# A gated-linear-attention, expert and GLU kernel on one core: attention products in float32 with turned outputs, other loads and another hand-over

## The chip, the core and the metric

The kernel runs on one core of a Trainium2 chip. The core has five engines with queues of their own, each of which runs its instructions in the order of the program: PE (TensorE: matrix products, whose weight loads are shown apart as PEld), DVE (VectorE), ACT (ScalarE), POOL (GpSimd) and SP (SyncE, which here only issues DMAs). The metric is the device time of one execution in microseconds (us), taken as the median of the runs.

## The reference, cut to what matters

```python
# gated linear attention: B=4, 8 heads, 768 steps, head size 48
f = 1.0 / (1.0 + np.exp(-f_logit))
for t in range(S):
    state = f[:, :, t, :, None] * state + np.einsum('bhd,bhe->bhde', k[:, :, t], v[:, :, t])
    y[:, :, t] = np.einsum('bhd,bhde->bhe', q[:, :, t], state)
x = y as 3072 tokens of 384
# one expert of 8 per token
e_idx = np.argmax(x @ w_gate, axis=1)
h = np.maximum(x[mask] @ w1[e], 0.0)          # 384 -> 1024
out[mask] = gate_w * eom * (h @ w2[e])        # 1024 -> 384
# a gated linear unit over all tokens
gate = 1.0 / (1.0 + np.exp(-(x @ w_gate)))    # 384 -> 1536
out = (gate * (x @ w_val)) @ w_out            # 1536 -> 384
```

## The kernel before

**Attention.** The tokens are cut into 24 units of 128 steps (`NU`, six to a batch). Queries, keys and decays arrive turned, with two heads down the partitions: rows 0 to 47 and 64 to 111 of a tile of 112 rows (`PD`), and four such pairs (`HP`) side by side. Per unit: `s_log` makes logarithms of the decays (ACT), `s_sum` their running sums (DVE, one scan per pair), `s_decay` the exponentials (ACT) and the products with keys and queries (`kT`, `qT`, on POOL). `s_part` and `s_part2` then cut keys and queries into a high and a low part of the type float32r, the queries of each head among zeros for the other head (`qbh`, `qbl`), so that `s_score` can make the scores of two heads at a time from three float32r products of 256 columns (units 0 to 2 take whole float32 tiles, `qw`, instead). `am` is the score under the causal mask. `s_turn` turns the keys (`pk`), `s_state` makes the chunk's addition to the state (`pM`, then `sn`), and `s_y` the output `pY` with tokens down the partitions: per head `am` by 48 columns of values, per pair `qT` by 96 columns of the state. `s_xt` turns the finished rows again (`px`) and `s_logit` makes the two sets of eight router logits (`plg`) from them. A float32 product stands in the trace as two weight loads and two MATMULs, a transposition as one.

**Routing.** After every group of tiles (`groups`) `route` finds each token's expert and its rank there with some twenty small DVE instructions, and `put_rows` writes the rows with indirect DMAs (POOL) to the experts' slots in DRAM (`xs_all`).

**Experts.** Nine passes: the early slots of expert 0 (`W0`), its other ones, then the seven other experts in the order of their loads, each with up to 512 tokens. A pass has eight units `f` of 128 hidden columns, each with nine products for `ph` and, two units later (`LAG`), nine for `po`, all in three float32r parts (`mm3`). SP loads the weights (`st`, three buffers), ACT and DVE split them (`w_hi`, `w_lo`) into a ring of slots that the expert before gives back. Beside this the weights of the last stage, which are doubles, are loaded (`stg`, by SP), rounded (`single`, on ACT, POOL and DVE) and split. At unit 1 of a pass `store_pass` copies the last pass's outputs (`yt`) and stores them; at unit 4 `put_ids` writes the token numbers (one element of 4 bytes per row) and `gather_rows` fetches rows for the pass after the next one.

**GLU.** Six groups of 512 tokens by twelve units; a unit has 18 products of 512 columns and 12 of 384. The outputs are scattered by indirect DMA.

The order on each engine is the order of the code (`manual_schedule`); the loop over `i` interleaves stages of several units, and the tile library sets the waits. The lines that the change touches are printed below.

Of the kernel before, what the change touches and what calls it, by code (L numbers as in the profile page):

```python
# [28 lines left out]
def kernel(  # L29
# [36 lines left out]
    EARLY = 18  # L66
    #: The first tile of the last group.
    LATE = 21
    #: The slots of expert 0 that the first EARLY tiles fill.
    W0 = 208  # L70
    #: The rows of a pair of heads: the second's start at half the partitions.
    PD = P // 2 + D
    NRING = 34
    NWARM = 16
    #: The units whose products take the keys and queries whole.
    WHOLE = 3
    #: The units from which the vector engine takes the keys' low parts.
    LOW = 21
    WARM = (2, 2)
    FILL = {-2: 2, -1: 4, 0: 4, 1: 2}  # L80
# [10 lines left out]
    id_all = drp.tile([NT + SLOT, 1], I32, name="id_all")  # L91
# [7 lines left out]
    wg16 = const.tile([P, KD, 2 * NE], F32, name="wg16")  # L99
    carry = const.tile([P, 1, NE], BF16, name="carry")  # L100
    #: Of each token: its number and its factor.
# [7 lines left out]
    flag = const.tile([1, 1], I32, name="flag")  # L109
    gc_all = const.tile([PD, NU, HP], F32, name="gc_all")  # L110
    bm = const.tile([PD, 2], F32, name="bm")
    zero = const.tile([P, 1], F32, name="zero")

    def constants():
# [4 lines left out]
        )  # L119
        nc.vector.tensor_tensor(out=tris, in0=tri, in1=ident, op=ALU.subtract)  # L120
        nc.vector.tensor_reduce(
            out=bm, in_=ident[0:PD, :].rearrange("p (j d) -> p j d", j=2), axis=AX.X, op=ALU.add
        )
        nc.vector.memset(onec, 1.0)
        nc.gpsimd.iota(e8[:, 0, :], pattern=[[-1, NE]], base=NE, channel_multiplier=0, allow_small_or_imprecise_dtypes=True)
        nc.vector.memset(carry, 0.0)
        # NT less a token's number: an empty slot's zeros stand for none.
        nc.gpsimd.iota(meta[:, :, 0].bitcast(I32), pattern=[[-P, NU]], base=NT, channel_multiplier=-1)
# [3 lines left out]
    def load_router():  # L132
        nc.sync.dma_start(wg16[:, :, 0:NE], moe_w_gate.rearrange("(k p) e -> p k e", p=P))
        nc.sync.dma_start(wg16[:, :, NE : 2 * NE], moe_w_output_gate.rearrange("(k p) e -> p k e", p=P))
# [4 lines left out]
    def choose(pool, lg, u0, n):  # L139
        """The expert of each token of n tiles (its one-hot row) and the token's factor."""  # L140
# [7 lines left out]
        nc.vector.tensor_reduce(out=m, in_=l, axis=AX.X, op=ALU.max)  # L148
        nc.vector.tensor_tensor(out=t, in0=l, in1=bc(m, NE), op=ALU.subtract)
        nc.scalar.activation(out=ex, in_=t, func=AF.Exp)  # L150
        nc.vector.tensor_tensor(out=sc, in0=l, in1=bc(m, NE), op=ALU.is_equal)
        nc.vector.tensor_tensor(out=sc, in0=sc, in1=e8b, op=ALU.mult)
        nc.vector.tensor_reduce(out=ms, in_=sc, axis=AX.X, op=ALU.max)
        nc.vector.tensor_tensor(out=oh, in0=sc, in1=bc(ms, NE), op=ALU.is_equal)

        factor = [
            lambda: nc.vector.tensor_tensor(out=ohf, in0=oh, in1=g, op=ALU.mult),
            lambda: nc.vector.tensor_reduce(out=sel, in_=ohf, axis=AX.X, op=ALU.add),
            lambda: nc.scalar.activation(out=eg, in_=sel, func=AF.Exp, scale=-1.0),
# [1163 lines left out]
```

## Time and profile before

| | us |
|---|---|
| median of 3 runs (1016.81 to 1018.68) | 1017.18 |
| span of the profiled execution | 1017.1 |
| PE busy in it | 976.9 (96%) |
| PE weight loads | 890.3 (88%) |
| DVE busy | 527.7 (52%) |
| ACT busy | 380.1 (37%) |
| POOL busy | 253.1 (25%) |

The profiled execution and the median agree to 0.1 us. Busy shares are means over stages of unlike kinds, and a busy PE may run at half its clock, so the stages have to be read one by one; PE's granted clock stands beside its busy time in the view of stretches.

### The profile page before, as it was taken

The page shows a single profiled execution, that of the slowest core. Times are in us where ns is not written, and L with a number is a line of the kernel's source. Part 1 is how long each engine was busy: PE and PEld are TensorE (multiplying, and loading weights), DVE is VectorE, ACT ScalarE, POOL GpSimd, SP SyncE. Part 2 cuts the span into 40 slices and gives each one's busy share as a digit, 9 for nine tenths or more (in the row PEclk, how much of TensorE's full clock was granted, in tenths as well). Part 3 has the DMA queues.
Part 4 walks back from the last instruction along what each step waited for, and adds up shares of the span by engine and source line. Part 5 has one row for each costly group of instructions (what it writes and reads, how often), then busy time and mean ns, then how long its engine had stood idle before and what let it go on. Part 6 is the DMA issues. An engine that isn't in the chain of part 4 may idle for free.

```text
span 1017.1 us, 13322 instructions
## 1 busy us (share of the span) xinstructions
PE 976.9 (96%) x4891; PEld 890.3 (88%) x4891; DVE 527.7 (52%) x1011; ACT 380.1 (37%) x729; POOL 253.1 (25%) x220
## 2 busy tenths in 40 slices
PE   8999999999998998989979999999999999999996
PEld 5899999999997787988978888888888888888886
DVE  8978867866344875777769723222223222222222
ACT  5655455443124554455535522222222122122211
POOL 6544354545110432434345200100100100100001
PEclk8755555555599899999999999999999999999999
DMA  8576454331167586576653200100100100000000
GB/s 196 173 242 197 125 154 133 93 107 55 45 137 162 163 223 162 132 245 205 209 118 111 92 1 1 63 1 1 63 1 1 63 1 1 32 1 5 27 1 34
DMA packets 57532, 96.00 MB, mean 94 GB/s; under 512 B 13258, under 2 KB 35186, under 8 KB 57458
## 3 DMA queue, kind: packets, MB, share of 16 engines
q1 hardware_dynamic: 54386, 85.60, 30.9%
q0 software_dynamic: 3072, 9.46, 2.4%
q8 instruction: 40, 0.66, 0.3%
q14 instruction: 34, 0.28, 0.1%
HBM read 68.35 MB, written 26.69 MB: 93 GB/s over the span
## 4 chain that ended last, share of the span: by engine, by line
issue 43%; PE 36%; DVE 7%; DMA 7%; ACT 3%; POOL 2%; SPq 0%; POOLq 0%; DVEq 0%; ACTq 0%
PE pY L586 6%; DMA st<-in_moe_w_dram 6%; PE pS L542 5%; PE pY L583 3%; PE plg L398 2%; PE ph L762 2%; PE pM L563 2%; PE ph L763 2%; PE ph L764 2%; PE po L762 2%; PE po L763 2%; PE po L764 2%; DVE w_lo L225 2%; POOL out_dram L964 2%; PE px L386 1%
## 5 line engine op out<-in xcount | busy, mean ns | idle before, releaser
L1082 DVE TENSOR_TENSOR hf<-pv,sg 128x512 f32<-128x512 f32 x72 | 49.8, 691 | 267.6 <-PE pv L764 266.5
L964 POOL DMA_INDIRECT out_dram<-ob,ids x24 | 23.6, 982 | 410.7 <-DVE ob L963 405.2
L1078 ACT ACTIVATE sg<-pg 128x512 f32<-128x512 f32 x72 | 43.0, 598 | 174.1 <-PE pg L764 174.1
L1085 ACT CAST hh<-hf 128x512 fp32r<-128x512 f32 x72 | 44.7, 621 | 160.3 <-DVE hf L1082 160.3
L225 DVE TENSOR_TENSOR w_lo<-st,w_hi 128x384 fp32r<-128x384 f32 (+1 forms) x112 | 78.2, 723 | 51.0 <-ACT w_hi L224 50.0
L763 PE MATMUL po<-w_lo,hh 128*128 128x384 f32 x288 | 97.1, 337 | 0.0
L762 PE MATMUL po<-w_hi,hh 128*128 128x384 f32 x288 | 97.0, 337 | 0.0
L764 PE MATMUL po<-w_hi,hl 128*128 128x384 f32 x288 | 96.8, 336 | 0.0
L762 PE MATMUL po<-hh,w_hi 128*128 128x208 f32 (+8 forms) x216 | 76.2, 353 | 19.4 <-ACT yt L935 16.4
L586 PE MATMUL pY<-v,am 128*128 128x48 f32 x384 | 89.2, 384 | 0.0
L586 PEld LDWEIGHTS pY<-v,am 128*128 128x128 f32 x384 | 88.6, 320 | 0.2
L763 PE MATMUL pg<-xt_lo,w_hi 128*128 128x512 f32 x216 | 85.3, 395 | 0.0
L762 PE MATMUL pg<-xt_hi,w_hi 128*128 128x512 f32 x216 | 85.0, 394 | 0.0
L764 PE MATMUL pg<-xt_hi,w_lo 128*128 128x512 f32 x216 | 85.0, 394 | 0.0
L763 PE MATMUL pv<-xt_lo,w_hi 128*128 128x512 f32 x216 | 85.0, 394 | 0.0
L762 PE MATMUL pv<-xt_hi,w_hi 128*128 128x512 f32 x216 | 84.9, 393 | 0.0
L764 PE MATMUL pv<-xt_hi,w_lo 128*128 128x512 f32 x216 | 84.8, 393 | 0.0
L224 ACT CAST w_hi<-st 128x384 fp32r<-128x384 f32 (+1 forms) x112 | 59.6, 560 | 66.9 <-DMA st<-in_moe_w_dram 52.5
L174 POOL TENSOR_SCALAR cva<-cva 128x512 f32<-128x512 f32 (+1 forms) x30 | 58.8, 1960 | 94.6 <-ACT cva L173 94.5
L762 PE MATMUL ph<-xt_hi,w_hi 128*128 128x208 f32 (+8 forms) x216 | 78.1, 362 | 2.9 <-DVE hl L1015 1.5
L763 PE MATMUL ph<-xt_lo,w_hi 128*128 128x208 f32 (+8 forms) x216 | 76.6, 355 | 0.0
L763 PE MATMUL po<-hl,w_hi 128*128 128x208 f32 (+8 forms) x216 | 74.8, 346 | 1.7 <-DVE hl L1015 1.7
(182 smaller groups left out, 2197.3 us busy)
## 6 DMA issues: line engine op xcount, KB each, us to landing
st<-in_moe_w_dram SPq DMA_DIRECT2D x48, 256.0 KB, 5.0
st<-in_moe_w_dram SPq DMA_DIRECT2D x32, 384.0 KB, 5.3
qk<-in_qkt_dram SPq DMA_DIRECT2D x48, 192.0 KB, 4.2
xs_all<-zrow SPq DMA_DIRECT2D x8, 772.0 KB, 4.9
yT_all<-zrow SPq DMA_DIRECT2D x21, 256.0 KB, 3.1
ft<-in_ft_dram SPq DMA_DIRECT2D x48, 96.0 KB, 4.6
v<-in_v_dram SPq DMA_DIRECT2D x24, 192.0 KB, 2.6
stg<-in_moe_w_gate_dram SPq DMA_DIRECT2D x9, 512.0 KB, 6.2
```

The costliest lines, as they stand in the source:

```text
L174: nc.gpsimd.tensor_scalar(out=af, in0=af, scalar1=HW_LEAST, scalar2=HW_MOST, op0=ALU.max, op1=ALU.min)
L224: nc.scalar.copy(hi, src)
L225: nc.vector.tensor_tensor(out=lo, in0=src, in1=hi.bitcast(F32), op=ALU.subtract)
L542: nc.tensor.matmul(pS[:, 2 * i : 2 * i + 2, :], lhsT=a, rhs=b, start=(n == 0), stop=(n == len(terms) - 1))
L586: nc.tensor.matmul(pY[:, h, :], lhsT=d["am"][:, h, :], rhs=vt[:, h, :], start=(c == 0), stop=True, skip_group_check=True,)
L762: nc.tensor.matmul(ps, lhsT=ah, rhs=bh, start=first, stop=False)
L763: nc.tensor.matmul(ps, lhsT=ah, rhs=bl, start=False, stop=False)
L764: nc.tensor.matmul(ps, lhsT=al, rhs=bh, start=False, stop=last)
L964: put = nc.gpsimd.indirect_dma_start(out=out[:, :], out_offset=bass.IndirectOffsetOnAxis(ap=idx[g][:, i : i + 1], axis=0), in_=ob, in_offs ...
L1078: nc.scalar.activation(out=sg, in_=pg, func=AF.Sigmoid)
L1082: nc.vector.tensor_tensor(out=hf, in0=pv, in1=sg, op=ALU.mult)
L1085: nc.scalar.copy(hh, hf)
```

## The change

The scores, the outputs and the state's part of them are now float32 products of one head each. `s_score` gives head `j` of a pair the rows 0 to 47 or 64 to 111 and a bank of its own; `s_y` makes the output turned (`pY[at, hp, :]`: 48 or 64 columns of weights from the values, 128 moving columns from `am`), so that its copy `xT` feeds the logits directly and `s_rows` turns it back for the rows. `s_part`, `s_part2` and their tiles go; `kT` moves from POOL to DVE; the scan is one instruction for all four pairs; the state is 48 columns per pair instead of 96. The start is written out, with units 0 and 1 ahead of the loop. `route` is cut into more steps, the groups are (6, 6, 5, 5, 2) tiles, and the rows for pass 0 are fetched, scaled and turned inside the attention loop. In the expert stage the staged loads go from three buffers to five (`NST`), the doubles are fetched from POOL's queue, the last addition of `single` goes from POOL to DVE, the stores of `yt` and of the token numbers come later and in pieces, and a token number is written with its row's last 16 words. The zero fills of `yT_all` and `id_all` and half of that of `xs_all` go.

```diff
     def route(u0, n):
...
+        some(first)
         yield
+        some(factor, 3)
+        yield
...
+    def s_rows(u):
+
+        px = bank_mm([P, HP, 2, P // 2], "px")
+        for hp in range(HP):
+            nc.tensor.transpose(
+                px[:, hp].rearrange("p j d -> p (j d)")[:, 0:PD], st[u]["xT"][:, hp, :], ident[0:PD, 0:PD]
+            )
...
+        pl = bank_po(MISC, [P, 2 * NE], "plg")
+        for hp in range(HP):
+            nc.tensor.matmul(pl, lhsT=d["xT"][:, hp, :], rhs=wgp[:, hp, :], start=(hp == 0), stop=(hp == HP - 1))
...
+            nc.vector.tensor_tensor_scan(
+                out=d["ls"].rearrange("p h t -> p (h t)"), data0=runs01.rearrange("p h t -> p (h t)"),
+                data1=d["ln"].rearrange("p h t -> p (h t)"), initial=0.0, op0=ALU.mult, op1=ALU.add,
+            )
...
+            nc.vector.tensor_tensor(out=kT, in0=tin["qk", u][:, 1], in1=gi, op=ALU.mult)
...
+        def s_score(u):
+
             d = st[u]
...
+            pS = [bank_mm([P, HP, P], "pS") for _ in range(2)]
+            for hp in range(HP):
+                for j in range(2):
+                    rows = slice(j * (P // 2), j * (P // 2) + D)
+                    nc.tensor.matmul(
+                        pS[j][:, hp, :], lhsT=d["kT"][rows, hp, :], rhs=d["qT"][rows, hp, :], start=True, stop=True
+                    )
...
+                        nc.tensor.matmul(
+                            pM[at, hp, :], lhsT=d["kt"][:, hp, at], rhs=tin["v", u][:, 2 * hp + j, :],
+                            start=True, stop=True,
+                        )
...
                     nc.tensor.matmul(
-                        pY[:, h, :], lhsT=d["am"][:, h, :], rhs=vt[:, h, :], start=(c == 0), stop=True,
-                        skip_group_check=True,
+                        pY[at, hp, :], lhsT=vt[:, h0 : h0 + at.stop - at.start], rhs=d["am"][:, j, hp, :],
+                        start=(hp == 0), stop=(c == 0), skip_group_check=True,
                     )
...
+            if c:
+                for hp in range(HP):
+                    for j in range(2):
+                        at = half(j)
+                        nc.tensor.matmul(
+                            pY[at, hp, :], lhsT=so[at, hp, :], rhs=d["qT"][at, hp, :], start=False, stop=True,
+                            skip_group_check=True,
+                        )
...
+            for i in range(1, NU):
+                if i == NU - 1:
+                    gather_rows(0)
+                s_score(i)
...
+                on(s_keys, i + 1)
+                on(s_queries, i + 1)
...
+                s_y(i - 1)
                 load("v", i + 4)
...
+                s_state(i)
+                on(s_turn, i + 1)
+                if i == LAST:
+                    scale(xg[0], passes[0][2], nc.vector)
+                    s_y(i)
+                if i > 16:
+                    step_route()
+                s_rows(i - 1)
+                s_logit(i - 1)
...
+            to_xt(0, xg[0], passes[0][2])
+            for todo in routing:
+                for _ in todo:
+                    pass
+            put_rows(6)
+            s_rows(LAST)
+            s_logit(LAST)
...
-                nc.sync.dma_start(st_, wo_w[key[1] * P : (key[1] + 1) * P])
+                nc.gpsimd.dma_start(st_, wo_w[key[1] * P : (key[1] + 1) * P])
...
-            nc.gpsimd.tensor_tensor(out=dst, in0=dst, in1=af, op=ALU.add)
+            nc.vector.tensor_tensor(out=dst, in0=dst, in1=af, op=ALU.add)
...
-    feed = Feed(3)
+    feed = Feed(NST)
```

On PE, in a unit in the middle of attention before (`pY` first of the state, then of the scores; `pS` begins the next unit):

```order
L583 MATMUL pY<-sn,qT 128x96
L586 MATMUL pY<-v,am 128x48 x2
L386 MATMUL px<-ident,x 128x128 x3
L563 MATMUL pM<-v,kt 112x96 x4
L398 MATMUL plg<-wg_76,xT 128x16 x3
L542 MATMUL pS<-qbh_121,kh 128x256
L542 MATMUL pS<-qbh_121,kl 128x256
L542 MATMUL pS<-qbl_122,kh 128x256
```

On PE, the same place after the change (the alternating rows of `pY` and of `pM` stand four times each, of which the last `pY` and the first `pM` pair are shown, and the last row of `pM` with what follows):

```order
L640 MATMUL pY<-am,v 64x128
L640 MATMUL pY<-am,v 48x128
L648 MATMUL pY<-qT,sn 48x128 x8
L615 MATMUL pM<-v,kt 64x48
...
L575 MATMUL pk<-ident,kT 128x112 x4
L487 MATMUL px<-ident,xT 128x112 x4
L498 MATMUL plg<-wgp,xT 128x16 x4
L587 MATMUL pS<-qT,kT 128x128 x8
```

The scores moved from twelve float32r products of two heads to eight float32 products of one head in one run, and the outputs have 128 moving columns where they had 48 and 96.

On SP, in the middle of a pass before (`put_ids`, the rows for a later pass, then weight loads and a load of doubles):

```order
L240 DMA st_4178<-in_moe_w_dram 128x2x384
L923 REGISTER_ALU
L923 DMA id_all<-xs 128x3x1
L923 ISA
L923 DMA id_all<-xs 40x1
L745 ISA
L745 DMA xs<-xs_all 128x3x386
...
L233 DMA st_4239<-in_moe_w_dram 128x512
L796 DMA stg<-in_moe_w_gate_dram 128x1024
```

On SP, a pass after the change, from the store of the outputs of the pass before to the rows for a later one:

```order
L964 DMA yT_all<-yt 128x3x424
L475 ISA
L475 DMA id_all<-xs 24x16
...
L246 DMA st_4676<-in_moe_w_dram 128x512
L475 ISA
L475 DMA id_all<-xs 128x3x16
L453 ISA
L453 DMA xs<-xs_all 128x2x386
```

The two writes of token numbers no longer follow each other, and the loads of doubles have left this queue.

On PE, between attention and the first expert product before (`xlate` are rows of the last tiles, `pw` products that keep PE busy, `ptx` the rows of pass 0):

```order
L398 MATMUL plg<-wg_76,xTlate 128x16 x3
L386 MATMUL px<-ident,xlate 128x128 x3
L291 LDWEIGHTS oneb
L291 MATMUL pw<-oneb 128x512
...
L716 MATMUL ptx<-ident,xs 128x128 x3
L716 MATMUL ptx<-ident,xs 128x80 x3
...
L762 MATMUL ph<-xt_hi,w_hi 128x208
```

On PE, the same place after:

```order
L498 MATMUL plg<-wgp,xT 128x16 x4
L424 MATMUL ptx<-ident,xs 128x128 x3
L424 MATMUL ptx<-ident,xs 128x64 x3
L330 LDWEIGHTS tris
...
L487 MATMUL px<-ident,xT 128x112 x4
L788 MATMUL ph<-xt_2354,w_hi 128x192
```

The filling products are gone there, and the rows of pass 0 are turned ahead of the last tile's own rows and logits.

## Rows read from the trace of the kernel before

**Rows 1.** Page, part 2: PE's granted clock in 40 slices.

```profile
PEclk8755555555599899999999999999999999999999
```

**Rows 2.** Stretches by stage: length, busy us (instructions) by engine, clock, DMA share, GB/s.

```profile
11.60:53.00 41.40, 37.05 (x221) 33.57 (x221) 40.00 (x64) 24.95 (x47) 25.58 (x21) 0.75 0.74 192
53.00:268.70 215.70, 214.42 (x1050) 214.26 (x1051) 152.51 (x310) 99.81 (x191) 93.06 (x85) 0.50 0.43 130
276.40:557.70 281.30, 257.10 (x1393) 237.75 (x1394) 194.60 (x384) 135.57 (x285) 92.44 (x62) 0.96 0.64 168
557.70:1010.50 452.80, 451.55 (x2162) 394.52 (x2160) 129.72 (x204) 110.80 (x191) 29.32 (x29) 1.00 0.06 21
```

**Rows 3.** Order of time, PE: start, length, line, product; starts of two units.

```profile
219.30 0.56 PE L542 MATMUL pS<-qbh,kh 112*128 112x256 f32 x1
231.08 0.56 PE L542 MATMUL pS<-qbh,kh 112*128 112x256 f32 x1
```

**Rows 4.** Order of time, PE: runs of one product while the clock is high.

```profile
11.58 1.13 PE L542 MATMUL pS<-qw,kT 112*128 112x256 f32 x4 [1.32 <-DVE qw L504]
...
13.55 1.04 PE L542 MATMUL pS<-qw,kT 112*128 112x256 f32 x4
14.43 0.94 PE L563 MATMUL pM<-v,kt 128*112 128x96 f32 x8
...
43.91 0.51 PE L386 MATMUL px<-ident,x 128*128 128x128 f32 x3
44.26 0.93 PE L563 MATMUL pM<-v,kt 128*112 128x96 f32 x8
45.02 0.77 PE L398 MATMUL plg<-wg,xT 128*128 128x16 f32 x6
45.64 0.37 PE L542 MATMUL pS<-qbh,kh 112*128 112x256 f32 x1
```

**Rows 5.** Short stretches around the changes of the clock.

```profile
15.00:20.00 5.00, 3.00 (x20) 2.08 (x19) 4.91 (x9) 2.84 (x5) 3.40 (x3) 0.97 1.09 246
...
40.00:45.00 5.00, 5.00 (x47) 5.00 (x47) 4.94 (x7) 3.52 (x8) 3.06 (x2) 0.98 0.78 227
...
50.00:55.00 5.00, 3.43 (x27) 3.05 (x26) 4.90 (x8) 3.83 (x7) 3.30 (x2) 0.88 0.98 278
55.00:60.00 5.00, 5.00 (x26) 5.00 (x25) 4.94 (x9) 1.68 (x3) 3.12 (x2) 0.50 0.93 300
```

**Rows 6.** Groups by line and shape, 100 to 240 us, DVE: busy us, mean ns.

```profile
L548 DVE TENSOR_TENSOR am<-pS,tri 128x512 f32<-128x512 f32 x25 | 17.3, 690 | 7.5 <-PE pS L542 7.3
L453 DVE TENSOR_TENSOR_SCAN ls<-ln,zero 112x128 f32<-112x128 f32 x48 | 16.3, 404 | 0.0
...
L225 DVE TENSOR_TENSOR w_lo<-st,w_hi 128x384 fp32r<-128x384 f32 x7 | 3.8, 545 | 0.0
...
L399 DVE COPY lg<-plg 128x16 f32<-128x16 f32 x12 | 2.0, 168 | 4.1 <-PE plg L398 4.1
L521 DVE TENSOR_TENSOR kl<-kT,kh 112x512 fp32r<-112x512 f32 x2 | 1.9, 942 | 0.0
L567 DVE TENSOR_TENSOR sn<-pM,gcm 112x384 f32<-112x384 f32 x2 | 1.1, 558 | 5.2 <-PE pM L563 5.2
L154 DVE TENSOR_TENSOR oh<-sc,ms_all 128x48 bf16<-128x48 f32 x3 | 0.6, 208 | 0.1
```

**Rows 7.** The same groups of ACT.

```profile
L463 ACT ACTIVATE gi<-ls 112x512 f32<-112x512 f32 x12 | 7.4, 615 | 0.0
```

**Rows 8.** The same groups of POOL.

```profile
L468 POOL TENSOR_TENSOR qT<-qk,ls 112x512 f32<-112x512 f32 x13 | 21.5, 1650 | 0.0
```

**Rows 9.** Order of time, PE: the first product of the experts and of the GLU.

```profile
276.41 0.52 PE L762 MATMUL ph<-xt_hi,w_hi 128*128 128x208 f32 x1
...
557.74 0.39 PE L762 MATMUL pg<-xt_hi,w_hi 128*128 128x512 f32 x1
```

**Rows 10.** Waits of PE, 420 to 480 us: us in total, times, longest.

```profile
PE po L762 <- ACT yt L935: 5.5, 2, 3.5
```

**Rows 11.** Waits of ACT, 420 to 480 us.

```profile
ACT w_hi L224 <- DMA st<-in_moe_w_dram: 14.1, 4, 6.4
```

**Rows 12.** Waits of SP's queue, 345 to 500 us.

```profile
SPq L923 <- DMA id_all<-xs: 37.7, 5, 9.0
```

More of the change, by code (lines that the diff above doesn't have):

```diff
@@ L110, with masks @@
     gc_all = const.tile([PD, NU, HP], F32, name="gc_all")
-    bm = const.tile([PD, 2], F32, name="bm")
-    zero = const.tile([P, 1], F32, name="zero")
-    def constants():
+    wgp = const.tile([PD, HP, 2 * NE], F32, name="wgp")
+    def masks():
         make_identity(nc, ident)
@@ L342, in route @@
             ]
[L343 to L346 removed]
+        some(factor, 1)
+        some(rank)
+        if u0 < SOON:
+            yield
+        some(factor)
         if u0 == EARLY:
@@ L358, in put_rows @@
             nc.gpsimd.tensor_copy(xrow[u][:, DM:XW].bitcast(I32), meta[:, u, :].bitcast(I32))
+        for u in puts[0:most]:
             put = nc.gpsimd.indirect_dma_start(
@@ L377, in put_rows @@
         del puts[0:most]
[L379 to L392 removed]
+    xts = {}
@@ new lines, with in_parts, new_xt @@
+    xg = {}
+    def in_parts(dst, j, src, w):
+        hi, lo = dst
+        nc.scalar.copy(hi[:, j, 0:w], src)
+        nc.vector.tensor_tensor(out=lo[:, j, 0:w], in0=src, in1=hi[:, j, 0:w].bitcast(F32), op=ALU.subtract)
+    def new_xt(key, w):
+        if key == 0:
+            both = xsp.tile([P, 2, KD, w], F32R, name="xt0", tag="xs")
+            pair = (both[:, 0], both[:, 1])
+        else:
+            pair = tuple(xtp.tile([P, KD, NB * P], F32R, name="xt_" + nm) for nm in ("hi", "lo"))
+        xts[key] = tuple(t[:, :, 0:w] for t in pair)
+        return pair
@@ new lines, with runs, gather_rows @@
+    passes = [(0, 0, W0), (0, W0, CAPS[0] - W0)] + [(r, 0, CAPS[r]) for r in range(1, NE)]
+    def runs(w):
+        n, z = divmod(w, P)
+        return [(0, n, P)] * bool(n) + [(n, 1, z)] * bool(z)
+    def gather_rows(p):
+        if p < len(passes):
+            r, s0, w = passes[p]
+            xs = xsp.tile([P, NB, XW], F32, name="xs", tag="xs")
+            for i, n, z in runs(w):
+                r0 = (who[r] * SLOT if r else s0) + i * P
+                get = nc.sync.dma_start(
+                    xs[0:z, i : i + n, :], xs_all[bass.ds(r0, n * z), :].rearrange("(b p) d -> p b d", p=z)
+                )
+                if p == 0:
+                    tc.declare_no_dep(get.ins, group="late rows", reason="other rows")
+                    assert len(early_puts) == EARLY
+                    for put in early_puts:
+                        tc.add_manual_dep(
+                            get.ins,
+                            put.name,
+                            mybir.DependencyInfo(mybir.DependencyClass.Sync, mybir.DependencyReason.DATA),
+                            reason="rows",
+                        )
+            xg[p] = xs
@@ L429, in load @@
         def load(nm, u):
-            if 0 <= u < NU:
+            if 0 <= u < NU and (nm, u) not in tin:
                 b, c = divmod(u, NCH)
@@ L555, with half @@
         sbd = {}
+        def half(j, wide=False):
+            return slice(j * (P // 2), j * (P // 2) + (P // 2 if wide and j == 0 else D))
         def s_state(u):
@@ L1033 @@
                     if planning:
-                        next(planning, None)
-                    elif next(routing, True):
+                        for _ in range(2):
+                            next(planning, None)
+                    elif i == 1:
+                        for _ in routing:
+                            pass
                         put_rows(6)
@@ L1111 @@
                     if f == 8 and g + 1 < NG:
-                        tok_parts(g + 1)
+                        for _ in tok_parts(g + 1):
+                            pass
     def general():
```

609 lines of the change are left out of this document (264 added, 345 removed).

## The prediction

> **What bounds the kernel now.** I read the clock line of the page first, then the stretches by stage, then single products in order of time, and last the waits. The clock line shows 2.4 GHz at the start, 1.2 GHz (5 tenths) from the third to the eleventh slice, and 2.4 GHz afterwards [rows 1]. The stretches put that beside the stages [rows 2]. Attention fills 11.6 to 268.7 us. From 53 us on PE is busy for 214.42 of 215.70 us at half clock; DVE (152.51), ACT (99.81) and POOL (93.06) all have room. So PE sets the pace: a unit starts at 219.30 and the next at 231.08, 11.78 us [rows 3]. The experts run from 276.41 to 557.74 us [rows 9], 281.3 us, in which PE is idle for 281.3 − 257.1 = 24.2 us and has a mean clock of 0.96; that mean says some 8% (22 us) at half speed, which costs half of it, 11 us [rows 2]. The GLU is 452.8 us of gapless products at full clock [rows 2], and 6.6 us of stores end the span of 1017.1 us. That span and the median of 1017.18 us agree, so the sum needs no correction.
>
> **Products of an attention unit after the change.** A float32 product stands in the trace as two MATMULs. At 2.4 GHz one MATMUL of 256 columns takes (14.43 − 13.55)/4 = 0.22 us, one of 128 columns (44.26 − 43.91)/3 = 0.117 us, so these go by moving columns; one of 96 columns takes (45.02 − 44.26)/8 = 0.095 us and one of 16 columns (45.64 − 45.02)/6 = 0.103 us, so these go by their weight loads of 112 to 128 columns [rows 4]. After the change a unit has 8 float32 products of 128 columns for the scores, 8 for `am` by values and 8 for the state's part: 48 MATMULs by 0.117 = 5.6 us. `pM` is 16 MATMULs with 48 or 64 columns of weights and 48 moving ones, which no row shows: between 0.095 (no gain from the smaller size) and half of that, 1.5 or 0.8 us. `pk` and `px`, 8 transpositions by 0.095 to 0.117, are 0.85 us, and `plg`, 8 by 0.103, is 0.83 us. One after the other that is 8.8 us. But the two heads of a pair use different rows or columns of the array, and products on different parts of it may run side by side; no row before shows such a pair. If all 48 and `pM` did, the unit would be 2.8 + 0.8 + 0.85 + 0.83 = 5.3 us. I take the middle, 7.0 us: weight loads, switches between the three ways of cutting the array and the first product of each run keep the gain from being whole.
>
> The Trainium skill, page "TensorEngine Tiling (Array Packing)", section "Key Properties", says that different tiles can load weights and multiply in parallel, and also that changing the tiling mode drains the engine. The first would put the unit at the lower end. The second speaks against this change, which changes mode about five times a unit; a drain as long as the tail of a run of `px` (0.51 − 3 × 0.117 = 0.16 us [rows 4], an estimate) would add 0.8 us a unit or 18 us in all. No run here shows either yet.
>
> **Other engines in a unit.** DVE: two masks by 0.69 (`am`), `kT` taken over from POOL by 0.94 (the row of `kl`, same size and operands), one scan for four, at most 4 × 0.404 = 1.62, taken 1.3 because three starts go; the state in half the columns, 0.3 of the 0.558 of `sn` and 0.4 for its second step; `lg` 0.17; 14 weight splits of about 0.6 over 23 rounds, 0.37; some 20 routing steps of 0.2 in five groups, 20/24 = 0.8. Sum 5.7 us [rows 6]. ACT: four exponentials and logarithms by 0.615, three copies of about 0.5 to 0.6, a small one and the splits, 4.7 us [rows 7]. POOL: `qT` 1.65 and a row's scatter, about 3.2 us [rows 8]. So below 6 us PE is no longer the bound and DVE is: there is 6.0 us at least. What goes with `s_part` and `s_part2` (on ACT, DVE and POOL) is worth nothing by itself, as none of these engines sets the pace now; it makes the room in which a faster PE can use its time.
>
> **The clock.** The price of the whole change hangs on 2.4 GHz in attention. It held through 15 to 20 us with PE busy for only 3.0 of 5 us, rose again by 40 to 45 us after a dense run with float32 scores, was lost after 50 to 55 us (3.43 of 5 us busy), and did not come back at 55 to 60 us or in the 200 us behind it, though PE was never idle [rows 2, 5]. The PE time that failed to raise it was mostly weight loads with 16 to 96 moving columns beside them. After the change 48 of some 80 MATMULs of a unit stream as long as their weights load or longer, in one run. So I expect the full clock for most of the stage.
>
> **Sum.** First score at 12 us (11.58 before [rows 4]; the start waits for the same loads, exponentials and scans). Unit 0 ahead of the loop 3.5 us, 3 us for slow first rounds (constants, zero fills), 23 rounds by 7.0 = 161 us, then the last unit's output, its rows and logits and the turning of pass 0's rows, 6 us: the first expert product comes at 185.5 us instead of 276.41 [rows 9], a gain of 91 us. This includes the end of the old hand-over, 7.7 us at half clock between 268.7 and 276.4 us, which the fetch inside the loop covers.
>
> Experts: 281.3 less 24.2 idle and 11 of clock is a floor of 246 us. The stalls: PE waits for `yt` on ACT, up to 3.5 us at a time [rows 10]; ACT stands before a `w_hi` whose load has not landed (14.1 us in four waits within 60 us [rows 11]); and SP, which should have issued that load, was held by the second write of token numbers, five times, up to 9.0 us each [rows 12]. The order on SP no longer puts those writes behind each other, and five buffers let loads run ahead. Against that, DVE takes the additions of `single`: 30 by 0.55 to 0.69, 18 us on top of 194.6 busy [rows 2, 6], so DVE would be at 213 of some 260 us, and its queue will still delay a few `hl`. I leave 16 of the 35 us of loss in place: 262 us, a gain of 19 us. Bounds: 250 (a few us left) and 281 (none gained). The GLU keeps its products, and its conversions are hidden beside 452.8 us of PE: nothing. The shorter zero fills and the moved loads are off the path: nothing, unless SP falls behind; loads would then need some 800 KB a unit in 7 us, 115 GB/s, under the 192 GB/s that 11.6 to 53 us already show [rows 2].
>
> 185.5 + 262 + 452.8 + 6.6 = **907 us**.
>
> **Rivals.**
> - *The halves overlap wholly* and DVE sets the pace: 6.0 us a round, 162.5 us to the first expert product, 884 us. For it: the operands lie in separate halves throughout, scores even in separate banks. Against: `pY` has both heads in one bank, and weights still load one after the other. Chance 0.18.
> - *The halves do not overlap*: 8.9 us a round, 24.5 + 205 = 229 us, 951 us. For it: no row shows two products at once. Chance 0.16.
> - *The clock stays at 1.2 GHz*: a round is 2 × 7.0 = 14 us, 24.5 + 322 = 346.5 us, **1068 us, slower**. The mechanism is what the trace shows at 53 us: one gap, then half clock to the end of the stage. It decides from 11.8 us a round on, where 24.5 + 23 T + 262 + 459.4 reaches 1017. Against it: the dense float32 runs, which precede the rise by 45 us. Chance 0.06, a sixth of it near no change.
> - *The expert stage gains nothing*, because DVE with its additions delays `hl` as the loads did: 926 us. Chance 0.05.
>
> **How the numbers follow.** The forecast as described has 0.55, with a range of its own from 885 to 930. 8 in 10 should lie between 868 (whole overlap, and 250 us of experts with a shorter start) and 952 (no overlap); outside are the low clock and sizes beyond the bounds. Faster by over 0.2% (about what a measurement of this kernel can tell from no change): 0.94, all cases but the low clock; within 0.2%: 0.01; slower: 0.05.
>
> **What would show it.** The clock line at 9 or 10 tenths in the attention slices; unit starts (`pS`) 6 to 8 us apart; 128-column `pY` and `pS` MATMULs starting about 0.06 to 0.12 us apart; the first `ph` near 185 us and the first `pg` near 448 us; no wait of SP for `id_all` over 2 us. A clock of 5 tenths, or starts over 11.8 us apart, makes the forecast wrong in kind; starts of 6 or 9 us make it wrong in size only.

## The result and the profile after

| | us |
|---|---|
| before, median of 4 runs (1016.81 to 1019.04) | 1017.93 |
| after, median of 4 runs (851.55 to 854.03) | 851.73 |
| ratio after / before, 95% interval | 0.8368 (0.8350 to 0.8386) |
| forecast (range) | 907 (868 to 952) |
| span of the profiled execution after | 849.8 |

The change is faster by 16.3%, which is more than the forecast of 907 us and lies below its range. The clock line of the page after (40 slices, tenths of 2.4 GHz), against [rows 1]:

```profile
PEclk9999999999999999999999999999999999999998
```

The half clock of attention is gone. The stretches by stage, with the columns of [rows 2]: attention from its third unit to the start of the last one, the hand-over, the experts, the GLU:

```profile
17.50:131.00 113.50, 111.68 (x1591) 99.19 (x1590) 97.14 (x211) 86.55 (x183) 56.85 (x55) 0.98 0.84 229
131.00:138.90 7.90, 7.90 (x109) 6.64 (x108) 4.00 (x16) 2.42 (x8) 0.00 (x0) 1.00 0.03 5
138.90:387.70 248.80, 245.41 (x1403) 232.15 (x1403) 204.70 (x426) 136.08 (x283) 77.64 (x72) 1.00 0.63 194
387.70:843.20 455.50, 452.85 (x2161) 393.27 (x2159) 133.11 (x217) 113.35 (x196) 27.26 (x27) 1.00 0.07 22
```

PE is idle for 1.8 us in the first of these and for 3.4 us in the experts (24.2 us before [rows 2]). The first products of the experts and of the GLU, in order of time on PE (start, length), where [rows 9] has 276.41 and 557.74 us:

```profile
138.91 0.36 PE L788 MATMUL ph<-xt,w_hi 128*128 128x192 f32 x1
387.67 0.39 PE L788 MATMUL pg<-xt_hi,w_hi 128*128 128x512 f32 x1
```

| stage | before | forecast | after | after − before |
|---|---|---|---|---|
| to the first expert product | 276.4 | 185.5 | 138.9 | −137.5 |
| experts | 281.3 | 262 | 248.8 | −32.5 |
| GLU and stores | 459.4 | 459.4 | 462.1 | +2.7 |
| span | 1017.1 | 907 | 849.8 | −167.3 |

One unit of attention after, in order of time on PE, from one `pS` to the next, 70.15 to 75.59 us, so 5.44 us against 11.78 [rows 3]:

```profile
70.15 1.16 PE L587 MATMUL pS<-qT,kT 48*128 48x128 f32 x16
71.24 1.09 PE L640 MATMUL pY<-am,v 128*64 128x128 f32 x16
72.26 1.08 PE L648 MATMUL pY<-qT,sn 48*48 48x128 f32 x16
73.26 0.67 PE L615 MATMUL pM<-v,kt 128*64 128x48 f32 x16
73.86 0.61 PE L575 MATMUL pk<-ident,kT 112*128 112x112 f32 x4
74.30 0.55 PE L487 MATMUL px<-ident,xT 112*128 112x112 f32 x4
74.69 0.98 PE L498 MATMUL plg<-wgp,xT 112*128 112x16 f32 x8
75.59 1.16 PE L587 MATMUL pS<-qT,kT 48*128 48x128 f32 x16
```

From start to start the 48 MATMULs of `pS` and `pY` take 1.09 + 1.02 + 1.00 = 3.11 us, `pM` 0.60, `pk` and `px` 0.83, `plg` 0.90. Units at the ends of a batch lack a run and are shorter; from the third `pS` (17.48 us) to the last (130.97 us) there are 21 rounds of 5.40 us.

The other engine that matters, DVE, in groups by line and shape from 30 to 120 us (busy us, mean ns, idle before), against [rows 6]:

```profile
L594 DVE TENSOR_TENSOR am<-pS,tri 128x512 f32<-128x512 f32 x34 | 21.8, 681 | 0.6 <-PE pS L587 0.3
L543 DVE TENSOR_TENSOR_SCAN ls<-runs,ln 112x512 f32<-112x512 f32 x17 | 20.9, 1232 | 0.7 <-POOL qT L563 0.2 <-ACT ln L536 0.2
L554 DVE TENSOR_TENSOR kT<-qk,gi 112x512 f32<-112x512 f32 x16 | 13.3, 832 | 0.2
L625 DVE TENSOR_TENSOR sn<-sn,gc_all 112x192 f32<-112x192 f32 x11 | 5.3, 481 | 0.4
```

### The profile page after: what moved, and what is told of

It reads as the page before. It is cut to its first block, busy times and chain, and to the rows that moved or that the text cites. A ratio compares the mean times of both kernels' runs of the same rounds, so it can differ in the third digit from the quotient of the medians.

```text
span 849.8 us, 14043 instructions
## 1 busy us (share of the span) xinstructions
PE 832.9 (98%) x5387; PEld 740.4 (87%) x5387; DVE 452.0 (53%) x896; ACT 350.9 (41%) x690; POOL 171.2 (20%) x171
## 3 DMA queue, kind: packets, MB, share of 16 engines
q1 hardware_dynamic: 44882, 62.97, 25.8%
## 4 chain that ended last, share of the span: by engine, by line
issue 50%; PE 37%; DMA 3%; DVE 3%; POOL 3%; ACT 2%; POOLq 0%; ACTq 0%; DVEq 0%; SPq 0%
PE ph L788 4%; PE po L788 4%; PE ph L789 4%; PE po L790 4%; PE ph L790 4%; PE po L789 4%; PE pY L640 2%; POOL out_dram L998 2%; PE pS L587 2%; PE pY L648 2%; DMA ft<-in_ft_dram 2%; PE plg L498 2%; PE ptx L424 1%; PE px L487 1%; DMA st<-in_moe_w_dram 1%
## 5 line engine op out<-in xcount | busy, mean ns | idle before, releaser
L1132 DVE TENSOR_TENSOR hl<-hf,hh 128x512 fp32r<-128x512 f32 x72 | 49.9, 693 | 49.4 <-ACT hh L1131 49.4
L238 DVE TENSOR_TENSOR w_lo<-st,w_hi 128x384 fp32r<-128x384 f32 (+1 forms) x112 | 69.2, 649 | 12.6 <-ACT w_hi L237 11.6
L788 PE MATMUL po<-hh,w_hi 128*128 128x192 f32 (+8 forms) x216 | 73.8, 341 | 0.0
L790 PE MATMUL po<-hh,w_lo 128*128 128x192 f32 (+8 forms) x216 | 73.7, 341 | 0.0
L789 PE MATMUL po<-hl,w_hi 128*128 128x192 f32 (+8 forms) x216 | 73.5, 340 | 0.0
L788 PE MATMUL ph<-xt_hi,w_hi 128*128 128x304 f32 (+7 forms) x192 | 68.0, 354 | 0.8 <-DVE hl L1049 0.8
L187 POOL TENSOR_SCALAR cva<-cva 128x512 f32<-128x512 f32 (+1 forms) x30 | 56.2, 1874 | 59.9 <-ACT cva L186 59.6
L1048 ACT ACTIVATE hh<-ph 128x192 fp32r<-128x192 f32 (+8 forms) x72 | 35.5, 493 | 78.0 <-PE ph L790 78.0
```

The costliest lines, as they stand in the source:

```text
L187: nc.gpsimd.tensor_scalar(out=af, in0=af, scalar1=HW_LEAST, scalar2=HW_MOST, op0=ALU.max, op1=ALU.min)
L238: nc.vector.tensor_tensor(out=lo, in0=src, in1=hi.bitcast(F32), op=ALU.subtract)
L788: nc.tensor.matmul(ps, lhsT=ah, rhs=bh, start=first, stop=False)
L789: nc.tensor.matmul(ps, lhsT=ah, rhs=bl, start=False, stop=False)
L790: nc.tensor.matmul(ps, lhsT=al, rhs=bh, start=False, stop=last)
L1048: nc.scalar.activation(out=hh, in_=pS, func=AF.Relu)
```

## The experiments

**Two theories on attention** were to be told apart first. Theory: the halves of the array work side by side, and a short unit at 2.4 GHz is the gain. Rivals: float32 scores alone bring the clock back and the rest matters little; or DVE sets the pace and PE's products matter little. The kernels ran in four groups, on chips on which the kernel before took 1020 to 1025 us (medians; 1018 us on the chip of the result), so ratios are compared between groups, and times within one.

### Heads one after the other

In the four runs of products the loops are turned round, so that neighbours use the same half of the array. The same products are made.

```diff
-            for hp in range(HP):
-                for j in range(2):
+            for j in range(2):
+                for hp in range(HP):
```

> The changed kernel with the two loops of the scores, the state and the outputs turned round: all four products of the first head of each pair, then all four of the second, so that neighbours in the queue use the same part of the array. The same 56 products, so the same MATMULs and bytes. Theory (the halves run side by side when neighbours use different parts): a run of 16 MATMULs of 128 columns goes from 1.09 to 16 x 0.117 = 1.87 us, three of them a unit, 2.4 us; pM adds some 0.2; a round goes from 5.2 to 7.7 us and the total from 852 to some 910 us. Rival (a MATMUL on half the array is shorter by itself, whoever stands beside it): no change, 852 us.

Measured: 891.34 us, ratio 0.8708 (0.8669 to 0.8747), span 884.8. The first expert product is at 173.68 us, 34.8 us later than after, and the span is 35.0 us longer. The order of time on PE, one unit (67.06 to 74.44 us, of which 0.27 us are routing's products in a place where the unit above has none):

```profile
67.06 1.71 PE L587 MATMUL pS<-qT,kT 48*128 48x128 f32 x16
...
68.97 1.57 PE L640 MATMUL pY<-am,v 128*64 128x128 f32 x16
70.47 1.55 PE L648 MATMUL pY<-qT,sn 48*48 48x128 f32 x16
71.95 0.83 PE L615 MATMUL pM<-v,kt 128*64 128x48 f32 x16
72.71 0.60 PE L575 MATMUL pk<-ident,kT 112*128 112x112 f32 x4
...
74.44 1.71 PE L587 MATMUL pS<-qT,kT 48*128 48x128 f32 x16
```

The runs of 16 now take 1.64, 1.50 and 1.48 us where they took 1.09, 1.02 and 1.00, and `pM` went from 0.60 to 0.76 us. Read start by start (medians of 15 to 21 units), two MATMULs of 128 columns on the same half follow each other by 0.109 to 0.112 us here. In the changed kernel the two halves start one each some 0.007 us apart, and such pairs follow each other by the same 0.109 to 0.112 us. So the overlap is shown, and inside a run it is whole; a MATMUL on half the array isn't shorter by itself.

But the edit undoes only a part of the overlap: PE starts the second head's first MATMUL beside the first head's fifth, ahead of three that stand before it in the code. The MATMULs of `pS` in flight (their ends are modelled) at 67.50, 67.86 and 68.40 us here:

```profile
67.27 0.49 PE L587 MATMUL pS<-qT,kT 48*128 48x128 f32 x3
67.60 0.49 PE L587 MATMUL pS<-qT,kT 48*128 48x128 f32 x5
68.16 0.49 PE L587 MATMUL pS<-qT,kT 48*128 48x128 f32 x3
```

And at 70.70 us in the changed kernel:

```profile
70.47 0.50 PE L587 MATMUL pS<-qT,kT 48*128 48x128 f32 x6
```

So 35 us are the least that the overlap is worth, and the round of 6.90 us on the mean (18.38 to 163.29 us, 21 rounds) isn't a round without overlap. No run has one; from the spacings I estimate 8.4 us a unit (24 pairs taken apart add 24 × 0.11 = 2.6 us to 5.44, `pM` adds 0.4).

### Twice the scan on DVE

The scan of all four pairs is made twice, 1.23 us more for DVE in each unit.

```diff
-            nc.vector.tensor_tensor_scan(
+            for _ in range(2):
+              nc.vector.tensor_tensor_scan(
```

> The changed kernel with the running sums made twice (the second scan writes the same numbers again): 1.23 us more of DVE a unit, 24 times. DVE is busy for 97 of the 113.5 us of the rounds, 4.4 us of 5.16 a round. Theory (PE sets the pace and DVE has 0.7 us of room a round): the first 0.7 us is hidden, the rest, about 0.5 us by 23 rounds, is paid: 852 + 12 = 864 us. Rival of the prediction (DVE sets the pace from 5.7 us on, and its queue is the path already): all of it is paid, 23 x 1.23 = 28 us, 880 us. Third: PE and DVE wait for DMA anyway, no change.

Measured: 878.56 us, ratio 0.8581 (0.8541 to 0.8621), span 876.0. The first expert product comes 25.8 us later. Stretches, first the 21 rounds from the third `pS` to the last, columns as above:

```profile
22.86:156.77 133.91, 121.88 (x1589) 107.32 (x1588) 126.11 (x232) 87.07 (x183) 61.15 (x55) 0.91 0.65 183
60.00:65.00 5.00, 3.07 (x39) 2.95 (x39) 4.90 (x11) 2.62 (x6) 0.00 (x0) 1.00 0.97 218
65.00:70.00 5.00, 5.00 (x60) 4.28 (x56) 4.96 (x6) 2.00 (x6) 1.35 (x1) 0.60 0.64 195
70.00:75.00 5.00, 4.99 (x33) 4.38 (x33) 4.26 (x11) 3.93 (x8) 1.48 (x1) 0.50 0.35 110
75.00:80.00 5.00, 4.91 (x68) 4.34 (x66) 4.83 (x12) 1.76 (x4) 0.00 (x0) 0.87 0.73 183
```

In the changed kernel DVE works 97.14 of 113.50 us, 4.63 us in each of 21 rounds (the expectation counted 22), so 0.77 us of a round looked free. Here a round takes 6.38 us, 0.97 more for 1.23 put in, so only some 0.26 us of it were used. By its size this is the rival's 880 us, but DVE's queue alone doesn't make it. 3.9 us stand ahead of the first score (13.44 against 9.56 us). Of the 20.4 us by which the 21 rounds grew, half is idle time of PE (12.0 against 1.8 us) and half is longer time for the same 1589 MATMULs, at a clock of 0.91 against 0.98. Routing's small steps come in bunches, and where they meet the second scan PE stands (3.07 us busy from 60 to 65 us), and behind it the clock is down. So a wait for DVE is paid here as idle time and again as clock, and little of DVE's idle time is room. The clock was back at 75 to 80 us, and no slice of that kernel's clock line lies under 7 tenths.

### Float32 scores alone, in the kernel before

All 24 units of the kernel before take whole float32 tiles for the scores, as its units 0 to 2 did.

```diff
-    WHOLE = 3
+    WHOLE = 24
```

> The kernel before with the whole float32 scores of its units 0 to 2 in all 24 units, nothing else: 8 MATMULs of 256 columns a unit in place of 12 float32r ones. Theory (the float32 products hold PE at 2.4 GHz in attention, the clock being most of the gain): the clock line shows 9 or 10 tenths in attention, a unit takes PE 5.8 + 0.4 = 6.2 us, DVE some 8 us with its copies of the queries, so that units come 8 us apart and the total falls by some 24 x 3.8 = 90 us to about 927 us. Rival (the clock needs the turned outputs, since products of 48 and 96 columns beside whole weight loads remain): clock at 5 tenths as before, units of about 13 us, total 1020 to 1050 us.

Measured: 1011.32 us median, but 984.11 to 1015.4 from run to run, with a mean clock of 0.886 to 0.914; the kernel before had 1024.68 us on that chip. Clock line and stretches, then the order of time on PE, where the brackets give the idle time before and what ended it:

```profile
PEclk9798555555799989999999999999999999999999
```

```profile
53.00:150.00 97.00, 93.19 (x535) 86.63 (x533) 78.33 (x189) 43.43 (x84) 33.37 (x30) 0.72 0.71 205
150.00:262.00 112.00, 112.00 (x488) 104.63 (x488) 60.06 (x179) 28.82 (x62) 38.00 (x47) 0.50 0.25 79
```

```profile
86.12 0.84 PE L398 MATMUL plg<-wg,xT 128*128 128x16 f32 x6 [1.37 <-DVE am L548]
...
94.07 1.10 PE L542 MATMUL pS<-qw,kT 112*128 112x256 f32 x4 [0.95 <-DVE am L548]
98.21 2.04 PE L542 MATMUL pS<-qw,kT 112*128 112x256 f32 x4
```

The clock lasted to some 95 us, where before it was gone at 55 us [rows 5]. Just ahead of that PE had waited for `am` on DVE (1.37 and 0.95 us). From there it ran at 1.2 GHz to the end of the stage, though it was busy for 112.00 of the last 112.00 us with long float32 runs among the products. Even the fastest run had a mean clock of 0.914, against 0.988 to 0.995 of the changed kernel. So float32 scores are not enough, and the prediction's explanation (streams as long as their loads bring the clock back) doesn't hold by itself.

### The same with the copies on ACT

To see whether the waits for DVE are what matters, the copies of the float32 queries go to ACT.

```diff
-                        nc.vector.tensor_copy(t[rows, :, j], d["qT"][rows, hf * (HP // 2) : (hf + 1) * (HP // 2)])
+                        nc.scalar.copy(t[rows, :, j], d["qT"][rows, hf * (HP // 2) : (hf + 1) * (HP // 2)])
```

> The kernel before with whole float32 scores in all units, and the copies of the queries that these need on ACT instead of DVE. In the run with the copies on DVE a unit took 6.2 us at 2.4 GHz until two waits of PE for `am` on DVE (1.4 and 0.95 us, at 85 to 94 us), after which the clock went to 1.2 GHz and stayed. The move takes 2.1 us a unit from DVE (of about 7) and gives it to ACT (about 4). Theory (gaps in PE's work cost the clock, and the products of the kernel before cannot win it back): fewer or later gaps, the clock holds through most of attention, the first expert product comes at 175 to 200 us and the total is 915 to 950 us. Rival (the product mix loses the clock sooner or later whatever the other engines do): half clock from about 100 us as before, total 990 to 1015 us.

Measured: 988.88 us median, 956.88 to 1029.76, with a mean clock between 0.868 and 0.945. In the profiled execution (span 955.2 us) the clock was lost and came back within the stage:

```profile
PEclk8965599989999998999899999999999999999999
```

With a lighter DVE the clock can come back within the stage, which it did not in the profiled execution with the copies on DVE; but it isn't held, and from run to run it comes and goes. On the cause this is inconclusive. What it shows is the price of an unsteady clock: the runs of this kernel lie 73 us apart (956.88 us at a mean clock of 0.945, 1029.76 us at 0.868), those of the changed one 2.5 us, and 4.2 us when it ran again.

### No filling products

The small products that only keep PE busy at the start are left out; they are no part of the output.

```diff
-    NWARM = 22
-    WARM = (2, 2, 2)
+    NWARM = 0
+    WARM = (0, 0, 2)
```

> The changed kernel without the 26 filling products of the start (none before the first scores, none between units 0 and 1). Theory (the products of a unit raise the clock by themselves): PE begins at 1.2 GHz, is raised within the first two or three rounds, and the total grows by no more than 5 us, to 857. Rival (the attention stage only keeps a clock that the start gave it): half clock to the end of attention, rounds of some 10 us, total near 960 us.

Measured: 854.88 us, ratio 0.8349 (0.8313 to 0.8385), against 0.8368 of after: no difference that can be told. Its granted clock was 1.00 over the first 20 us, so it didn't begin at 1.2 GHz as expected, and it stayed at 9 tenths in every slice. So the filling products aren't what holds the clock here.

### The loads of the experts, one piece at a time

The second question was why the experts gained 32.5 us and not 19. In this group the changed kernel ran again unaltered, beside three that undo one piece each: three staging buffers; both writes of token numbers at one place; the doubles' loads on SP's queue again. The three edits, in this order:

```diff
-    NST = 5
+    NST = 3
...
                         put_ids(p + 1, 0)
-                        ids_left = p + 1
+                        put_ids(p + 1, 1)
...
-                nc.gpsimd.dma_start(st_, wo_w[key[1] * P : (key[1] + 1) * P])
+                nc.sync.dma_start(st_, wo_w[key[1] * P : (key[1] + 1) * P])
```

> The changed kernel once more, unaltered, beside the three that follow on the same chip, so that differences of a few us are read against it. Every theory expects 852 us to within the spread of chips (the kernel before was 1018 us on one chip and 1025 us on another).

> The changed kernel with three staging buffers instead of five, so that weight loads run three ahead as before the change; the GLU's output copies share these buffers. Theory (the order on SP's queue was the stall, not the depth): loads still issue in time, 0 to 3 us more than the unaltered one. Rival (the depth was it): ACT stands before `w_hi` for some 14 us in 60 again and PE loses 3 to 5 us a pass, 15 to 20 us more.

> The changed kernel with both writes of a pass's token numbers one after the other, ahead of the fetch of rows, as before the change, but still 16 words a row. Theory (the second write holds SP until the first has landed, and that is what starved the weight loads): SP waits for the token numbers four to nine times, several us each; with five buffers ahead PE loses less than before the change, 5 to 10 us more in all. Rival (five buffers cover such a wait wholly, or the wider rows made the write quick): 0 to 2 us more.

> The changed kernel with the doubles of the last stage loaded from SP's queue again. Such a load waits for a buffer that DVE and ACT still read, and weight loads stand behind it. Theory (this blocking is a second share of the expert stage's gain): 4 to 8 us more. Rival (the waits are short, as the rows of the kernel before show 1.8 us at most for one): 0 to 2 us more.

| | median us (range) | passes 2 to 8, us |
|---|---|---|
| unaltered | 853.75 (852.89 to 857.12) | 207.5 |
| three buffers | 857.39 (854.98 to 861.03) | 207.5 |
| numbers together | 854.73 (851.57 to 856.09) | 207.5 |
| doubles on SP | 851.63 (849.99 to 853.93) | 207.3 |
| (before) | 1020.05 | 239.4 |

Passes 2 to 8 are counted from the first `ph` of 512 columns to the first `pg`, which leaves out what attention did. None of the three matters alone; the 3.6 us of three buffers don't lie in these passes, and the ranges overlap.

### All of them together, and the halves of that

This kernel has all three edits, and beside them writes the numbers as elements of 4 bytes again and puts the stores of `yt` back behind their copies:

```diff
-    IW = 16
-    ID0 = XW - IW
+    IW = 1
+    ID0 = DM
...
+            put_pass(p)
```

> The changed kernel with five pieces of the expert stage undone at once: three staging buffers, the doubles on SP's queue, both writes of token numbers together, one element of 4 bytes a row in them, and the outputs stored at once. Undone one by one, the first three cost +3.6, -2 and +1 us, and passes 2 to 8 kept their 207.5 us. Theory (the pieces stand in for one another, and together they are the 32 us by which passes 2 to 8 shrank from 239.4 us): passes 2 to 8 take 225 to 240 us, total 872 to 886 us. Rival (the gain came from elsewhere, from the addition on DVE, the later splits or the spread turning of the tokens): 207 to 212 us for these passes, total 852 to 860 us.

Measured: 891.88 us, ratio 0.8715 (0.8677 to 0.8753); passes 2 to 8 take 238.8 us, all of what before lost. So the pieces act on one loss: three of them, undone singly, cost nothing that shows in these passes, and all five together cost all of it. Two more runs halve the set, on one chip: the diff just above with the second of the three edits (the token numbers: 4 bytes, together, stores in their old place), and the first and third edit (the loads: three buffers, doubles on SP).

> Undone of the changed kernel: the token numbers alone (4-byte numbers again, both parts of a pass written one behind the other, and read back right behind the stores). Five staging buffers and POOL's queue for the double experts stay. Theory A, the loads are late because SP stands before the second write of numbers: SP holds some 45 to 50 us again, but five buffers let loads run ahead over one wait of 9 us; passes 2 to 8 (first ph of pass 2 to the first pg) take 215 to 228 us instead of 207.5, and the kernel comes to 862 to 875 us. Theory B, the numbers alone make the whole loss: passes 2 to 8 take 236 to 240 us and the kernel 885 to 893 us. Theory C, the numbers cost nothing without the short buffers: 207 to 209 us and 852 to 856 us.

> Undone of the changed kernel: three staging buffers instead of five and the double experts' loads on SP's queue again; the token numbers stay as changed. Theory A: with no long wait on SP the fewer buffers cost little, passes 2 to 8 take 207.5 to 211 us and the kernel 855 to 860 us. Theory B (numbers alone make the loss): the same, so this run tells A and B only from D. Theory D, buffers and queue make the loss whatever SP waits for: passes 2 to 8 at 225 to 240 us, the kernel at 872 to 893 us.

Measured: the numbers alone 871.4 us (866.19 to 872.31), passes 2 to 8 in 183.85 to 408.45 = 224.6 us; the loads alone 851.93 us (850.25 to 854.78), 182.56 to 389.98 = 207.4 us. Waits of SP's queue, then of PE, in the experts of the kernel with the old numbers (us in total, times, longest):

```profile
SPq L475 <- DMA id_all<-xs: 50.7, 6, 10.0
```

```profile
PE ph L788 <- DVE hl L1050: 9.3, 5, 3.0
```

And the stretch of its experts:

```profile
137.60:408.40 270.80, 257.57 (x1402) 242.33 (x1402) 202.60 (x424) 135.05 (x283) 76.09 (x71) 0.96 0.71 178
```

Theory A of these two expectations holds: SP stands 50.7 us before the second write of numbers, and the loads behind it are late (ACT waits 15.2 us for `st`, in the changed kernel not at all). Five buffers cover half of that (+17 us in passes 2 to 8); three, with the doubles on SP's queue, cover none of it (+31 us). Without the wait, three buffers do as well as five. The kernel with the numbers together but in rows of 64 bytes shows the same wait at a length that does no harm:

```profile
SPq L475 <- DMA id_all<-xs: 19.6, 6, 4.3
```

So the elements of 4 bytes belong to the loss. They were not undone alone, and neither was the place of the `yt` stores.

### The token numbers apart, in the kernel before

The reverse: before, with the second write of token numbers moved to unit 2 of the next pass as in after, still with 4 bytes and three buffers.

```diff
-            for i, n, z in runs(w):
+            for i, n, z in runs(w)[at : at + 1]:
...
-                        put_ids(p + 1)
+                        put_ids(p + 1, 0)
+                        ids_left = p + 1
```

> The kernel before with the second write of a pass's token numbers moved to unit 2 of the next pass, nothing else. SP waited 37.7 us for such writes between 345 and 500 us. Theory (this wait alone starved the weight loads): no wait of SP for token numbers over 2 us, ACT no longer stands before `w_hi` for 14 us in 60, passes 2 to 8 fall from 239.4 to 215 or less, total 20 to 25 us lower. Rival (with three buffers the loads come too late anyway, because SP also waits for their release and for the doubles): 5 us or less.

Measured: 1007.53 us, ratio 0.9856 (0.9798 to 0.9915); passes 2 to 8 fall from 239.4 to 222.5 us. That lies between the theory (215 us or less) and its rival. SP's wait for `id_all` went from 44.8 us in six waits to none, and PE's wait for `yt` on ACT from 16.4 to 1.3 us. So the wait on SP is about half of the loss there too. The other 15 us are not settled: ACT still waits 52.6 us for `st` in this kernel, as before (52.5 us). What differs from the kernel with the old loads but new numbers (207.4 us) is the 64-byte rows, the place of the `yt` stores and the additions of `single` on DVE, which were not taken apart.

## Why the prediction was right and wrong

**What bounds the kernel** was read rightly: PE at 1.2 GHz in attention [rows 1 to 3] and a late load chain in the experts [rows 10 to 12]. Both went. The GLU with its tail came to 462.1 instead of 459.4 us; these 2.7 us weren't taken apart.

**The step that failed is the unit's time on PE.** I worked out 8.8 us for products in a row and 5.3 us for whole overlap, and took the middle, 7.0 us. The full unit is 5.44 us, the mean round 5.40: whole overlap was right, and its terms with it (3.11 measured for 2.8, 0.60 for 0.8, 0.83 for 0.85, 0.90 for 0.83). The reasons for a middle (weight loads, switches, first products) had no row behind them, and they are small: 24 pairs by 0.11 us are 2.64 of the 3.11 us, so the ends of the three runs cost 0.47 us, where I had left 1.7 us a unit for all of them. From unit 1's scores (12.32 us) to the first expert product 126.6 us passed, where the forecast had 167: 40.4 of the 57 us by which the span is shorter than forecast. The upper end isn't tested: the kernel with heads apart keeps a part of the overlap, and the estimate from its spacings, 8.4 us, is near my 8.8 (the rival took 8.9). That its round of 6.90 us is near the forecast of 7.0 is chance.

**The second failed step is DVE's floor.** I put "6.0 us at least" beside a sum of 5.7 us. That shut the true case out: the rival of whole overlap was priced at 884 us for it, and the range's low end of 868 rests on it. DVE is busy for 4.63 us a round. The single terms were near (two masks 1.36 us for 1.38, the scan 1.23 for 1.3, `kT` 0.83 for 0.94, the state 0.83 for 0.7). The sum failed in three places. The terms were some 0.5 us too long together, since the means of all 211 instructions in the 21 rounds add up to 108.3 us, 5.16 a round. Neighbours on DVE overlap in the trace, so that these 108.3 us are 97.1 us of busy time, another 0.5 us a round. And I rounded a sum that was already high upwards by 0.3 us. 23 rounds by 0.6 us are 14 of the 16 us by which the time missed the range. With 5.4 us in place of 6.0, and the other two low bounds, the low end would have been 854 us.

**Smaller terms of attention.** The first score came at 9.56 us instead of 12, unit 0 took 2.76 instead of 3.5 us, and the slow first rounds, for which I had put 3 us, didn't occur (the second takes 5.16 us). Together 6.2 us.

**The experts.** The mechanism was right and its size was not. I left 16 of 35 us of stalls in place, because DVE with 18 us of additions would delay `hl`. DVE is busy for 204.7 of 248.8 us, and PE waits 0.8 us for `hl`: that fear had no ground. Two remedies for one cause (the writes apart and short, and more buffers) left nothing of the loss, 248.8 us, just below my bound of 250 and 2.8 us above the floor of 246. No wait of SP for `id_all` over 2 us was to be left; the one that is, 3.2 us, is the read of the token numbers for the last stage, not a write ahead of a load.

**The clock.** That it would hold was right. In one place after the change it fell, from 110 us on, where PE was idle for 0.35 us, and it was whole again from 120 us on:

```profile
110.00:115.00 5.00, 4.65 (x60) 3.92 (x57) 4.61 (x16) 4.67 (x12) 4.52 (x6) 0.90 0.70 185
115.00:120.00 5.00, 5.00 (x62) 4.41 (x59) 4.97 (x9) 1.87 (x4) 4.54 (x6) 0.76 0.24 87
120.00:125.00 5.00, 5.00 (x78) 4.44 (x78) 4.57 (x9) 3.88 (x9) 4.52 (x6) 1.00 0.23 82
```

My reason for it is not shown: the kernel before with float32 scores had the long runs and lost the clock. What in the new unit brings the clock back, the turned outputs, the overlap, or the lack of waits on DVE, stays open. Heads one after the other, with a part of the overlap gone, kept it too (0.98); with two scans and 12.0 us of idle time in the rounds it was 0.91.

**Side by side, and the switches.** The Trainium skill, page "TensorEngine Tiling (Array Packing)", section "Key Properties", says that tiles load weights and multiply in parallel; this trace agrees, 1.09 against 1.64 us for the same 16 MATMULs. The two weight loads of a pair start some 0.007 us apart too, so my "weights still load one after the other" was wrong. The other rule of that section of the Trainium skill, a drain at each change of mode, was estimated at 0.8 us a unit. No run isolates it. At a change the first MATMUL of the next run starts 0.15 to 0.20 us after the last one of the run before, 0.08 to 0.11 us more than inside a run; at five changes that is some 0.5 us a unit, and how much of it is a drain stays open.

**By what did attention gain, then?** Before, while the clock was at 2.4 GHz, a unit's first score stood at 45.64 us [rows 4] and the next unit's, in order of time on PE, here:

```profile
51.49 0.36 PE L542 MATMUL pS<-qbh,kh 112*128 112x256 f32 x1
```

That is 5.85 us, but this unit turns no keys. The unit at 219.30 us [rows 3] does, in 0.74 us:

```profile
220.72 0.95 PE L491 MATMUL pk<-ident,kT 112*128 112x112 f32 x4
221.46 0.61 PE L583 MATMUL pY<-sn,qT 112*128 112x96 f32 x2
```

So the same products take 5.85 us at 2.4 GHz and 11.78 − 0.74 = 11.04 us at 1.2 GHz, and a whole unit at 2.4 GHz would be some 6.2 us (an estimate, 5.85 + 0.74 × 5.85 / 11.04). Of the 6.4 us that a unit gained, some 5.5 are the clock and 0.8 the shorter unit. The change pays above all by the clock, which held in every run of the changed kernel (851.55 to 854.03 us, mean clock 0.988 to 0.995). That it holds because PE is seldom held up is likely, but not shown.

## What to carry to other kernels

Where a stage is at half clock, first compare the same unit at full clock in the same trace: the difference is the prize, and a change may win it even if its products are hardly shorter. Make sure that the two units have the same products. Products on opposite halves of the array, issued in turn, ran here at twice the rate inside a run; order the loop so that neighbours are on different halves. An experiment that undoes an overlap has to be looked at start by start, as it may undo only a part. When several remedies aim at one wait, undo them together before calling any of them useless: each one may cover for the rest.

## What the runs showed of the hardware

- Write and element size: the numbers of 384 rows took 7.9 us (median of five) to land as elements of 4 bytes, and 3.3 us as rows of 64 bytes, sixteen times the bytes. The issues in the experts of before and of after (KB each, us to landing):

```profile
id_all<-xs SPq DMA_DIRECT2D x5, 1.5 KB, 7.9
```

```profile
id_all<-xs SPq DMA_DIRECT2D x5, 24.0 KB, 3.3
```

- MATMULs of 128 columns on the same half of the array follow each other by 0.109 to 0.112 us, and so do pairs of them on opposite halves. In the kernel with heads apart PE started MATMULs on one half while three of the eight that stand before them in the code, on the other half, had yet to start. In `pM`, with 48 columns to move, each half keeps a pace of its own: 0.058 us with 64 columns of weights, 0.045 us with 48.
- The two losses of the clock shown above in kernels with the new attention lasted some 3 us (changed kernel) and 10 us (two scans), by the clock shares of their stretches. In the kernel before with float32 scores it stayed at 1.2 GHz for over 100 us, while PE was busy without a gap. The difference lies in what PE does, or when; no run here tells which.
